# Windowed attention with expert routing: score columns outside a batch written by TensorE, gate product with the weights stationary

## The chip, the cores and the metric

One core of a Trainium2 chip runs the whole program in one launch. The core has TensorE (PE; its weight loads are listed apart, as PEld), VectorE (DVE), ScalarE (ACT), GpSimd (POOL) and SyncE (SP), which issues most transfers. The metric is the time of one execution on the device, in microseconds (us).

## The reference

Three stages follow each other. In the first, 4 batches of 8 heads attend over 576 positions, each position to itself and the 127 before it:

```python
scores = scale * np.matmul(q, k.transpose(0, 1, 3, 2))          # scale = 1/8, head_dim 64
mask = (rel >= 0) & (rel < 128)                                  # rel = query position - key position
scores = np.where(mask, scores + bias[None], -1000000000.0)      # bias = -slope[h] * |rel|
scores = scores - np.max(scores, axis=-1, keepdims=True)
attn = np.exp(scores); attn = attn / (np.sum(attn, axis=-1, keepdims=True) + 1e-09)
return np.matmul(attn, v)
```

In the second, each of the 2304 tokens (512 numbers) goes to two of 8 experts, chosen by a gate:

```python
noisy_logits = x @ w_gate + np.log1p(np.exp(x @ w_noise)) * noise   # w_gate, w_noise: 512 x 8
top2 = np.argpartition(-noisy_logits, 2, axis=1)[:, :2]             # weights: softmax over the two
out[mask] += top2_w[mask, k, None] * (np.maximum(x[mask] @ w1[e], 0.0) @ w2[e])
```

The third is `r = max(x @ w_in, 0)`, then `(r * r) @ w_out`, with 2048 columns in between.

## The kernel before, in words

**The attention stage** works on 18 tiles of 128 tokens (number i). A tile holds two blocks of 64 queries (x = 0, 1), and there are 9 blocks in a batch. A tile is done in two steps, g = 0 and 1, of four heads each (two pairs j of two heads a), which gives 36 steps, v = 2i + g. A step does this:

- `s_step`: TensorE writes the scores of 64 queries against up to 192 keys into a pair of PSUM banks (psb, L256). VectorE adds the bias and takes the row extremes, with the sign turned, in one operation per head (L266, with a small read of the accumulator behind it). ScalarE takes the exponential (L272).
- `t_step`: TensorE transposes the result (L283, into psa), ScalarE copies it out (L285).
- `pv_step`: TensorE multiplies by V (L307, into psb). VectorE divides by the row sums (`norm`, L318, L321, L324).

**At the edge of a batch** the first block has 64 keys and the second 128, not 192. A tile that holds such a block is treated by `parts`: VectorE fills the unused columns of the result with 1e9 (L262), and the operation L266 runs for each half of the partitions by itself, eight times in a step and not four. This concerns tiles 0, 4, 5, 9, 13 and 14, thus 12 of the 36 steps: v = 0, 1, 8 to 11, 18, 19 and 26 to 29.

**The order** is written out by hand. The loop runs `s_step(v + 2)`, `t_step(v + 1)`, the work of slot 4, `pv_step(v)` with `norm`, then the work of slot 5. Slots 0 to 3 lie between the four maxima of a step. Every engine takes its instructions in this order. The banks of psb exist twice and are taken in turn by scores and by products with V, so the scores of a step can start only when the maxima of the step before have been read.

**The gate** works on pairs of tiles (p = 0 to 8), one pair every four steps. `gate_t` transposes the tokens of a tile (L337, into the single bank psc, copied out by L339), `gate_m` multiplies them by the gate's weights, with the tokens as the stationary operand (L347: 8 products of fp32, 16 records in the trace). ScalarE and VectorE work out the noisy logits (L351 to L360), the two largest (L363, L366) and their one-hot rows (L370). `rank` counts the tokens ahead on TensorE (L382), `place` turns the counts into places (L392 to L418), and `scatter` writes the tokens' numbers to those places by indirect transfers from POOL (L424).

**The end of the stage**: the places of tiles 12 and 13 (p = 6) must be scattered before a first part of the table is read back (L497) and the first 3 x 128 rows of expert 0 are gathered (L437) and transposed (L444). In the meantime TensorE works through the last steps. Experts and feed-forward stage follow; their code is not touched.

Of the kernel before, what the change touches and what calls it, by code (L numbers as in the profile page):

```python
# [11 lines left out]
F32 = mybir.dt.float32  # L12
# [31 lines left out]
C_TRI = C_BIAS + H * 192  # L44
C_N = C_TRI + 128


@with_exitstack
def attn_moe_ffn(ctx: ExitStack, tc: tile.TileContext, qt, kt, vt, wgn, noise, w1, w2, w_in, w_out,
# [81 lines left out]
    bias = qp.tile([128, H, 192], F32, name="bias")  # L131
    wg_sb = qp.tile([128, 4, 16], F32, name="wg_sb")
    nz_sb = qp.tile([128, NT, 8], F32, name="nz_sb")
    trs = qp.tile([128, 128], F32, name="trs")
    tri = const.tile([128, 128], BF16, name="tri")
    ones = const.tile([128, 128], BF16, name="ones")
    acc = const.tile([128, 2, 8], BF16, name="acc")
    snap = const.tile([1, 2, 4], F32, name="snap")
# [67 lines left out]
    load_v(4)  # L206
    nc.gpsimd.memset(ones, 1.0)
    nc.gpsimd.memset(acc, 0.0)
    nc.gpsimd.memset(zero, 0)
    nc.gpsimd.dma_start(out=slot_tab, in_=zero)  # L210

    def more_consts():
        nc.vector.tensor_copy(iota8, cst[:, C_IO:C_IO + 8])
        nc.vector.tensor_copy(tok, cst[:, C_TOK:C_TOK + NT])
        nc.vector.tensor_copy(tri, trs)

# [12 lines left out]

    def parts(i):  # L230

        c = [max(128 - 64 * ((2 * i + x) % TB), 0) for x in range(2)]
        if c == [0, 0]:
            return [(0, 128, 0)]
        return [(0, 64, c[0]), (64, 128, c[1])]

    def s_step(v, now):
# [7 lines left out]
        ps = bank("b")[:, :, 0:384].rearrange("p a (j n) -> p a j n", j=2)  # L245
        p2, mx = [], []
        for j in range(2):
            p2.append(wk.tile([128, 2, 192], F32, name="p2", tag="p2", bufs=6))
            mx.append(wk.tile([128, 2], F32, name="mx", tag="mx", bufs=6))
            for x in range(2):  # L250
                b, t = divmod(2 * i + x, TB)
                k0 = max(64 * t - 128, 0)
                n = 64 * t + 64 - k0
                for a in range(2):
                    pa = slice(64 * a, 64 * a + 64)
                    nc.tensor.matmul(ps[64 * x:64 * x + 64, a, j, 192 - n:192],  # L256
                                     Q[i][pa, 2 * g + j, 64 * x:64 * x + 64], K[b][pa, 2 * g + j, k0:k0 + n],
                                     start=True, stop=True)
        for p0, p1, c0 in parts(i):
            if c0:  # L260
                for j in range(2):
                    nc.vector.memset(p2[j][p0:p1, :, 0:c0], 1.0e9)  # L262
        for j in range(2):
            for a in range(2):
                for p0, p1, c0 in parts(i):
                    nc.vector.tensor_tensor_reduce(  # L266
                        out=p2[j][p0:p1, a, c0:], in0=ps[p0:p1, a, j, c0:], in1=bias[p0:p1, 4 * g + 2 * j + a, c0:],
                        op0=OP.add, op1=OP.min, scale=-0.125, scalar=3.0e38, accum_out=mx[j][p0:p1, a:a + 1])
                run(now, 2 * j + a)
# [63 lines left out]
    def gate_t(i):  # L333
        ps = bank("c").rearrange("p (c n) -> p c n", c=4)
        xi = XI.pop(i)
        for c in range(4):
            nc.tensor.transpose(ps[:, c, :], xi[:, c * 128:(c + 1) * 128], ident)  # L337
        G["xt", i] = wk.tile([128, 4, 128], F32, name="xt", tag="xt", bufs=4)
        nc.scalar.activation(out=G["xt", i], in_=ps, func=AF.Copy)  # L339


    def gate_m(p):
        gp = bank("c")[:, 0:32].rearrange("p (q w) -> p q w", q=2)
        for q in range(2):
            xt = G.pop(("xt", 2 * p + q))
            for c in range(4):
                nc.tensor.matmul(gp[:, q, :], xt[:, c, :], wg_sb[:, c, :], start=(c == 0), stop=(c == 3))  # L347
        gs = wk.tile([128, 8, 2, 8], F32, name="gs", tag="gs", bufs=2)
# [38 lines left out]
    def place(p, n):  # L387
# [21 lines left out]
        elif n == 4:  # L409
            for q in range(2):  # L410
                for k in range(2):
                    nc.vector.tensor_tensor_reduce(out=gs[:, 6 + k, q], in0=oh[:, q, k, :], in1=t[:, q],
                                                   op0=OP.mult, op1=OP.max, scale=1.0, scalar=0.0,
                                                   accum_out=pf[:, q, k:k + 1])
        elif n == 5:
# [90 lines left out]
    for p in range(NT // 2):  # L506
# [3 lines left out]
        at(v + 1, 4, gate_t, 2 * p + 1)  # L510
        at(v + 2, 0 if end else 4, gate_m, p)
        o = v + 2 if end else v + 3
# [658 lines left out]
def _consts():  # L1171
    c = np.zeros((128, C_N), np.float32)
    c[:, C_ID:C_ID + 128] = np.eye(128)
    c[:, C_TRI:C_TRI + 128] = np.arange(128)[:, None] < np.arange(128)[None, :]
    r = np.arange(64)
    col = np.arange(192)
# [14 lines left out]
def _layout(inputs):  # L1191
# [8 lines left out]
    vt = np.stack([vp[:, 64 * s:64 * s + 128] for s in range(10)], axis=2)  # L1200
    wgn = np.concatenate([f["moe_w_gate"], f["moe_w_noise"]], axis=1).reshape(4, 128, 16).transpose(1, 0, 2)
    noise = f["moe_noise"].reshape(NT, 128, 8).transpose(1, 0, 2)
# [22 lines left out]
```

## Time and profile before

| | |
|---|---|
| time, three runs | 1016.82, 1016.60, 1014.82 us; median 1016.6 |
| span of the profiled execution | 1016.9 us, 0.3 above the median and 0.1 above the slowest of the runs |
| PE busy | 975.9 us (96%) |
| PEld busy | 895.6 us (88%) |
| DVE busy | 696.9 us (69%) |
| ACT busy | 465.3 us (46%) |
| POOL busy | 381.8 us (38%) |
| mean granted TensorE clock | 0.986 of 2.4 GHz |

The shares are means over the whole span. The change touches the attention stage alone, which ends at about 159 us, where TensorE turns to the experts' products. What matters is therefore read from stretches of that stage: how long TensorE takes from one step's scores to the next, and whom it waits for.

### The profile page before, as it was taken

Reading aid. Unit: us, or ns where it says so; the run is one execution under the profiler, and the core shown is the slowest. Engines: PE = TensorE matmul, PEld = TensorE weight load, DVE = VectorE, ACT = ScalarE, POOL = GpSimd, SP = SyncE. Lnnn points to the kernel's source line nnn. Section 1 sums busy time; section 2 is a strip of 40 time slices with the busy share of each in tenths; the row PEclk is TensorE's granted clock in tenths of the full one; section 3 lists DMA queues with packets and bytes.
Section 4 is the critical chain, followed back from the end, with each engine's and each line's share of the span. In section 5 each row is a group of like instructions: output and inputs, shape, how many; then the busy total and the mean of one; then the engine's idle time right before and its main releaser. Section 6 shows DMA issues by size and latency. Waiting matters only on the chain. (4 is left out here: it accounts for less than half of the span.)

```text
span 1016.9 us, 19557 instructions
## 1 busy us (share of the span) xinstructions
PE 975.9 (96%) x7432; PEld 895.6 (88%) x7432; DVE 696.9 (69%) x1608; ACT 465.3 (46%) x857; POOL 381.8 (38%) x374
## 2 busy tenths in 40 slices
PE   8899789999999999999999999999999989999998
PEld 5677668989898989989898897999999978999997
DVE  5777854547667566756765266887577899887773
ACT  5677652334434343433443245655554454443331
POOL 1544443212121031312121033625121649988880
PEclk9999998999999999999999999999999999999999
DMA  9676532465656574574645253765634653444431
GB/s 315 209 241 229 160 116 74 146 186 148 204 170 206 173 248 157 193 232 165 204 149 178 85 173 94 229 177 166 168 101 140 193 166 105 145 135 140 134 112 42
DMA packets 135733, 168.04 MB, mean 165 GB/s; under 512 B 9856, under 2 KB 96016, under 8 KB 135248
## 3 DMA queue, kind: packets, MB, share of 16 engines
q1 hardware_dynamic: 128160, 145.98, 45.6%
q0 software_dynamic: 7472, 20.76, 6.6%
q8 instruction: 59, 0.97, 0.4%
q14 instruction: 42, 0.34, 0.1%
HBM read 118.69 MB, written 48.01 MB: 164 GB/s over the span
## 5 line engine op out<-in xcount | busy, mean ns | idle before, releaser
L272 ACT ACTIVATE p<-p,mx 128x192 f32<-128x192 f32 x144 | 60.4, 452 | 45.8 <-DVE mx L266 44.0
L815 POOL TENSOR_TENSOR gs<-xb 128x256 f32<-128x256 f32 x72 | 71.1, 1007 | 16.4 <-DVE wc L815 7.8
L472 ACT ACTIVATE ha<-psa 128x384 fp32r<-128x384 f32 x64 | 31.3, 491 | 98.6 <-PE psa L468 97.1
L633 POOL TENSOR_TENSOR ex<-ex 128x512 f32<-128x512 f32 x16 | 20.8, 1301 | 146.4 <-DVE ex L631 146.4
L633 POOL TENSOR_TENSOR et<-ex,et 128x512 f32<-128x512 f32 x16 | 20.9, 1305 | 137.7 <-DVE ex L631 137.7
L473 DVE SCALAR_TENSOR_TENSOR ha<-psa,ha 128x384 fp32r<-128x384 f32 x64 | 35.3, 554 | 47.2 <-ACT ha L472 46.9
L654 POOL DMA_INDIRECT yr<-yg,pos x36 | 38.8, 1078 | 73.3 <-DVE ha L473 52.2
L266 DVE CUSTOM_DVE_ANT_0 p<-psb,bias 128x192 f32<-128x192 f32 (+3 forms) x192 | 58.2, 319 | 9.7 <-PE psb L256 7.5
L424 POOL DMA_INDIRECT slots<-tok,pos x36 | 35.2, 977 | 73.4 <-DVE rs L318 46.3
L468 PE MATMUL psa<-xa,wa 128*128 128x384 f32 x288 | 54.4, 338 | 0.3 <-DVE ha L473 0.3
L468 PE MATMUL psa<-xa,wc 128*128 128x384 f32 x288 | 53.1, 335 | 0.0
L734 PE MATMUL psb<-wa,ha 128*128 128x512 f32 x216 | 53.0, 396 | 0.0
L738 ACT ACTIVATE yo<-psb 128x512 f32<-128x512 f32 x38 | 22.7, 597 | 61.5 <-PE psb L734 41.3
L468 PEld LDWEIGHTS psa<-xa,wa 128*128 128x128 f32 x288 | 49.6, 189 | 1.4 <-DVE ha L473 0.6
L468 PEld LDWEIGHTS psa<-xa,wc 128*128 128x128 f32 x288 | 49.6, 188 | 0.2
L815 DVE TENSOR_TENSOR wc<-gs,wc 128x512 fp32r<-128x512 f32 x48 | 48.7, 1054 | 1.3 <-ACT wc L815 1.3
L734 PE MATMUL psb<-wb,ha 128*128 128x512 f32 x176 | 46.3, 397 | 0.0
L734 PEld LDWEIGHTS psb<-wa,ha 128*128 128x128 f32 x216 | 39.5, 188 | 7.7
L114 DVE TENSOR_TENSOR wa<-raw,wa 128x1024 fp32r<-128x1024 f32 x20 | 24.5, 1224 | 30.2 <-ACT wa L110 30.2
L437 POOL DMA_INDIRECT xr<-xd,gidx x40 | 38.4, 960 | 16.9 <-issue 10.9
L473 DVE SCALAR_TENSOR_TENSOR hb<-psa,hb 128x512 fp32r<-128x512 f32 x32 | 22.1, 691 | 32.7 <-ACT hb L472 32.7
L992 DVE SCALAR_TENSOR_TENSOR yo<-yo 128x384 f32<-128x384 f32 x48 | 43.2, 900 | 1.6
(302 smaller groups left out, 2724.9 us busy)
## 6 DMA issues: line engine op xcount, KB each, us to landing
raw<-in_w_dram SPq DMA_DIRECT2D x64, 512.0 KB, 5.4
xb<-gmid SPq DMA_DIRECT2D x72, 256.0 KB, 3.4
v<-in_vt_dram SPq DMA_DIRECT2D x20, 520.0 KB, 5.1
yg<-yo SPq DMA_DIRECT2D x40, 256.0 KB, 4.3
gmid<-yo SPq DMA_DIRECT2D x48, 192.0 KB, 2.1
ex<-in_w_in_dram SPq DMA_DIRECT2D x16, 512.0 KB, 4.9
ex<-in_w_out_dram SPq DMA_DIRECT2D x16, 512.0 KB, 4.3
xd<-xi SPq DMA_DIRECT2D x18, 256.0 KB, 2.6
```

The source lines that it names most:

```text
L266: nc.vector.tensor_tensor_reduce(out=p2[j][p0:p1, a, c0:], in0=ps[p0:p1, a, j, c0:], in1=bias[p0:p1, 4 * g + 2 * j + a, c0:], op0=OP.add, ...
L272: nc.scalar.activation(out=p2[j][:, a, :], in_=p2[j][:, a, :], func=AF.Exp, bias=mx[j][:, a:a + 1], scale=-1.0)
L424: st = nc.gpsimd.indirect_dma_start(out=slots, out_offset=bass.IndirectOffsetOnAxis(ap=pos[:, i, k:k + 1], axis=0), in_=tok[:, i:i + 1], i ...
L437: nc.gpsimd.indirect_dma_start(out=XR[e, j], out_offset=None, in_=xd[0:EARLY * 128] if early else xd, in_offset=bass.IndirectOffsetOnAxis( ...
L468: nc.tensor.matmul(o, w[wp][:, f * 128:(f + 1) * 128], x[:, xp, d, :], start=(n == 0), stop=(n == 11))
L472: nc.scalar.activation(out=hi, in_=ps, func=AF.Relu)
L473: nc.vector.scalar_tensor_tensor(out=lo, in0=ps, scalar=0.0, in1=hi.bitcast(F32), op0=OP.max, op1=OP.subtract)
L633: nc.gpsimd.tensor_tensor(out=cf, in0=af, in1=cf, op=OP.add)
L654: nc.gpsimd.indirect_dma_start(out=YR[i, k], out_offset=None, in_=yg, in_offset=bass.IndirectOffsetOnAxis(ap=pos[:, i, k:k + 1], axis=0))
L734: nc.tensor.matmul(py, h[:, hq], wc[wp][:, wsl], start=(f + n == 0), stop=(f == 7 and n == 2))
L815: f(**a)
L992: nc.vector.scalar_tensor_tensor(out=t, in0=t, scalar=0.0, in1=t, op0=OP.max, op1=OP.mult)
```

## The change

Three edits. **Score columns**: at the edge of a batch TensorE writes the unused columns too, by products of bfloat16 constants (64 rows of ones against columns of -1.25e8, thus -8e9 in each), two for each such block. VectorE no longer fills anything, and L266 runs over all 128 partitions and 192 columns in every step, four times. **Gate**: the weights, padded from 16 to 32 columns, become the stationary operand. Each of the four quarters of the 512 inputs goes to its own group of 32 columns of the array (`gate_w`, 256 tokens at a time), so that the four partial sums come out side by side on 128 partitions. VectorE copies them to SBUF, and `gate_m` adds them up with a product against a constant 128 x 16 matrix, which brings the tokens back to the partitions. `gate_w` stands in slot 4, where `gate_m` was, and `gate_m` in slot 5, behind the product with V. **Places**: the four fused multiply-and-maximum operations of `place` become one product and one maximum over 32 elements.

```diff
@@ tiles
-    wg_sb = qp.tile([128, 4, 16], F32, name="wg_sb")
+    wg_sb = qp.tile([128, 4, 32], F32, name="wg_sb")
-    trs = qp.tile([128, 128], F32, name="trs")
+    trs = qp.tile([128, 144], F32, name="trs")
+    far = qp.tile([128, 256], BF16, name="far")
...
+    nc.gpsimd.memset(far, -1.25e8)
@@ s_step
-    def parts(i):
-        c = [max(128 - 64 * ((2 * i + x) % TB), 0) for x in range(2)]
-        if c == [0, 0]:
-            return [(0, 128, 0)]
-        return [(0, 64, c[0]), (64, 128, c[1])]
...
+        for x in range(2):
+            c = max(128 - 64 * ((2 * i + x) % TB), 0)
+            if c:
+                for a in range(2):
+                    pa = slice(64 * a, 64 * a + 64)
+                    nc.tensor.matmul(ps[64 * x:64 * x + 64, a, :, 0:c], ones[pa, 0:64],
+                                     far[pa, 0:2 * c].rearrange("p (j n) -> p j n", j=2), start=True, stop=True)
...
-        for p0, p1, c0 in parts(i):
-            if c0:
-                for j in range(2):
-                    nc.vector.memset(p2[j][p0:p1, :, 0:c0], 1.0e9)
         for j in range(2):
             for a in range(2):
-                for p0, p1, c0 in parts(i):
-                    nc.vector.tensor_tensor_reduce(
-                        out=p2[j][p0:p1, a, c0:], in0=ps[p0:p1, a, j, c0:], in1=bias[p0:p1, 4 * g + 2 * j + a, c0:],
-                        op0=OP.add, op1=OP.min, scale=-0.125, scalar=3.0e38, accum_out=mx[j][p0:p1, a:a + 1])
+                nc.vector.tensor_tensor_reduce(
+                    out=p2[j][:, a, :], in0=ps[:, a, j, :], in1=bias[:, 4 * g + 2 * j + a, :],
+                    op0=OP.add, op1=OP.min, scale=-0.125, scalar=3.0e38, accum_out=mx[j][:, a:a + 1])
@@ gate_t, gate_w, gate_m
-        G["xt", i] = wk.tile([128, 4, 128], F32, name="xt", tag="xt", bufs=4)
-        nc.scalar.activation(out=G["xt", i], in_=ps, func=AF.Copy)
+        p, q = divmod(i, 2)
+        if q == 0:
+            G["xt", p] = wk.tile([128, 4, 2, 128], F32, name="xt", tag="xt", bufs=2)
+        nc.scalar.activation(out=G["xt", p][:, :, q, :], in_=ps, func=AF.Copy)
+
+    def gate_w(p):
+        xt = G.pop(("xt", p)).rearrange("p c q n -> p c (q n)")
+        ps = bank("c")[:, 0:256]
+        for c in range(4):
+            nc.tensor.matmul(ps[32 * c:32 * c + 32, :], wg_sb[:, c, :], xt[:, c, :], start=True, stop=True)
+        G["gt", p] = wk.tile([128, 256], F32, name="gt", tag="gt", bufs=1)
+        nc.vector.tensor_copy(G["gt", p], ps)
 
     def gate_m(p):
         gp = bank("c")[:, 0:32].rearrange("p (q w) -> p q w", q=2)
+        gt = G.pop(("gt", p))
         for q in range(2):
-            xt = G.pop(("xt", 2 * p + q))
-            for c in range(4):
-                nc.tensor.matmul(gp[:, q, :], xt[:, c, :], wg_sb[:, c, :], start=(c == 0), stop=(c == 3))
+            nc.tensor.matmul(gp[:, q, :], gt[:, q * 128:(q + 1) * 128], trs[:, 128:144], start=True, stop=True)
@@ place, n == 4
-            for q in range(2):
-                for k in range(2):
-                    nc.vector.tensor_tensor_reduce(out=gs[:, 6 + k, q], in0=oh[:, q, k, :], in1=t[:, q],
-                                                   op0=OP.mult, op1=OP.max, scale=1.0, scalar=0.0,
-                                                   accum_out=pf[:, q, k:k + 1])
+            prod = gs[:, 6:8].rearrange("p k q w -> p q k w")
+            nc.vector.tensor_tensor(out=prod, in0=oh, in1=t[:, :, None, :].to_broadcast([128, 2, 2, 8]), op=OP.mult)
+            nc.vector.tensor_reduce(out=pf, in_=prod, op=OP.max, axis=mybir.AxisListType.X)
@@ slots of the pairs
         at(v, 4, gate_t, 2 * p)
         at(v + 1, 4, gate_t, 2 * p + 1)
-        at(v + 2, 0 if end else 4, gate_m, p)
+        at(v + 2, 0 if end else 4, gate_w, p)
+        at(v + 2, 0 if end else 5, gate_m, p)
@@ constants: column sums of the four groups; gate weights padded to 32 columns
+    c[:, C_SUM:C_SUM + 16] = np.arange(128)[:, None] % 32 == np.arange(16)[None, :]
...
+    wgn = np.zeros((128, 4, 32), np.float32)
+    wgn[:, :, 0:8] = f["moe_w_gate"].reshape(4, 128, 8).transpose(1, 0, 2)
+    wgn[:, :, 8:16] = f["moe_w_noise"].reshape(4, 128, 8).transpose(1, 0, 2)
```

How the order of instructions moves is shown at three places. The first is VectorE at step v = 10 (tile 5, the first block with 128 of its 192 keys): p2_792 and p2_798 are the two results, psb_791 the scores, mx the row extremes. Before:

```order
L262 MEMSET p2_792 64x2x64
L262 MEMSET p2_798 64x2x64
L266 ISA p2_792,mx_793<-psb_791,bias_93 64x128
L266 ISA mx_793 64x1
L266 ISA p2_792,mx_793<-psb_791,bias_93 64x192
L266 ISA mx_793 64x1
L266 ISA p2_792,mx_793<-psb_791,bias_93 64x128
L266 ISA mx_793 64x1
L266 ISA p2_792,mx_793<-psb_791,bias_93 64x192
L266 ISA mx_793 64x1
```

These are the two fills and the first half of the maxima; as many follow for p2_798. With the change the same step has the whole of its maxima in eight rows:

```order
L264 ISA p2_778,mx_779<-psb_775,bias_93 128x192
L264 ISA mx_779 128x1
L264 ISA p2_778,mx_779<-psb_775,bias_93 128x192
L264 ISA mx_779 128x1
L264 ISA p2_784,mx_785<-psb_775,bias_93 128x192
L264 ISA mx_785 128x1
L264 ISA p2_784,mx_785<-psb_775,bias_93 128x192
L264 ISA mx_785 128x1
```

Two fills, four maxima and four reads of the accumulator are gone from this step. The second place is TensorE around the gate of the first pair, from the scores of step v = 7 to those of step v = 8 (xt: transposed tokens; wg_sb: the weights; x8 counts products). Before:

```order
L256 MATMUL psb<-k,q 64x192 x8
L283 MATMUL psa<-cst,p_481 128x128 x3
L283 MATMUL psa<-cst,p_487 128x128 x3
L347 MATMUL psc<-wg_sb,xt 128x16 x8
L307 MATMUL psb<-v,pt 64x65 x16
L256 MATMUL psb<-k,q 64x192 x2
```

And with the change, up to the same scores:

```order
L259 MATMUL psb<-k,q 64x192 x8
L281 MATMUL psa<-cst,p_475 128x128 x3
L281 MATMUL psa<-cst,p_481 128x128 x3
L346 MATMUL psc<-xt,wg_sb 32x256 x4
L305 MATMUL psb<-v,pt 64x65 x16
L354 MATMUL psc<-trs,gt 128x16 x2
L248 LDWEIGHTS ones
L248 MATMUL psb<-far,ones 64x2x128
L248 LDWEIGHTS ones
L248 MATMUL psb<-far,ones 64x2x128
L259 MATMUL psb<-k,q 64x192 x2
```

Eight products of 16 columns are replaced by four of 256 columns in front of the product with V and two of 16 columns behind it, and the fills of an edge step stand ahead of its scores. The third place is VectorE in the same step with the change: gt_576 is the copy of the partial sums, the rows above it are the last two maxima of the step, those below the division by the row sums.

```order
L264 ISA p2_545,mx_546<-psb_538,bias_93 128x192
L264 ISA mx_546 128x1
L348 COPY gt_576<-psc_571 128x256
L316 TENSOR_SCALAR rs_595<-psb_578 128x4
L319 RECIPROCAL rs_595<-rs_595 128x4
L322 TENSOR_TENSOR xi_533<-psb_578,rs_595 128x256
```

The copy is new, behind the maxima of its step and ahead of the division; before, VectorE went from the one to the other.

## Rows read from the trace of the kernel before

**Rows 1.** Busy time by stretch; columns: stretch, length, busy by engine, PEclk, DMA share, GB/s

```profile
...
31.40:51.20 19.80, 15.31 (x246) 11.99 (x239) 17.32 (x111) 10.69 (x25) 8.94 (x11) 0.91 0.50 163
72.10:85.18 13.08, 11.95 (x180) 9.52 (x181) 10.50 (x69) 9.59 (x24) 7.57 (x10) 0.87 0.46 143
88.52:102.63 14.11, 13.75 (x251) 11.18 (x251) 9.80 (x72) 10.70 (x29) 7.63 (x10) 1.00 0.80 278
102.63:126.44 23.81, 18.57 (x284) 14.51 (x287) 19.24 (x122) 15.52 (x39) 10.89 (x17) 0.93 0.51 153
36.50:39.90 3.40, 3.12 (x32) 2.35 (x30) 3.07 (x18) 1.70 (x5) 0.00 (x0) 0.50 0.51 206
149.10:159.30 10.20, 7.13 (x53) 5.66 (x53) 4.15 (x22) 2.76 (x5) 4.59 (x9) 0.50 0.24 72
175.00:1016.90 841.90, 821.49 (x5164) 771.83 (x5163) 579.06 (x824) 360.71 (x595) 311.18 (x273) 1.00 0.52 160
...
```

**Rows 2.** Timeline of TensorE, four regular steps: start, length, engine, line, operation

```profile
...
88.52 0.88 PE L256 MATMUL psb<-k,q 64*64 64x192 f32 x16 [0.17 <-PE psb L307]
...
91.74 0.83 PE L256 MATMUL psb<-k,q 64*64 64x192 f32 x16
...
95.95 0.83 PE L256 MATMUL psb<-k,q 64*64 64x192 f32 x16
...
99.30 0.88 PE L256 MATMUL psb<-k,q 64*64 64x192 f32 x16
...
```

**Rows 3.** Waits of TensorE, 0 to 165 us: total, times, longest

```profile
...
PE psb L256 <- DVE mx L266: 5.5, 7, 1.7
PE psc L382 <- DVE oh L370: 5.3, 7, 2.2
PE psa L444 <- DMA xr<-xd,gidx: 3.1, 1, 3.1
...
```

**Rows 4.** VectorE groups up to 240 us: busy, mean ns, idle before

```profile
...
L266 DVE CUSTOM_DVE_ANT_0 p<-psb,bias 128x192 f32<-128x192 f32 (+3 forms) x192 | 58.2, 319 | 9.7 <-PE psb L256 7.5
...
L266 DVE DVE_READ_ACCUMULATOR2_ANT mx<- 64x1 f32 (+1 forms) x192 | 15.4, 80 | 0.0
...
L262 DVE MEMSET p<- 64x256 f32 (+1 forms) x32 | 6.8, 218 | 0.8
...
```

**Rows 5.** VectorE groups up to 165 us, shapes apart

```profile
...
L266 DVE CUSTOM_DVE_ANT_0 p<-psb,bias 128x192 f32<-128x192 f32 x96 | 30.7, 352 | 2.4 <-PE psb L256 2.0
L324 DVE TENSOR_TENSOR xi<-psb,rs 128x256 f32<-128x256 f32 x36 | 15.3, 425 | 1.3
...
L266 DVE DVE_READ_ACCUMULATOR2_ANT mx<- 128x1 f32 x96 | 8.0, 83 | 0.0
...
L412 DVE CUSTOM_DVE_ANT_0 gs<-oh,gs 128x8 f32<-128x8 bf16 x32 | 3.4, 162 | 0.3
...
L370 DVE TENSOR_TENSOR oh<-iota,sel 128x32 bf16<-128x32 uint32 x9 | 1.7, 190 | 0.1
...
```

**Rows 6.** TensorE groups up to 165 us, shapes apart

```profile
...
L256 PE MATMUL psb<-k,q 64*64 64x192 f32 x448 | 30.1, 350 | 4.8 <-DVE mx L266 2.6 <-DMA q<-in_qt_dram 1.6 <-PE psb L307 0.2
...
L256 PE MATMUL psb<-k,q 64*64 64x64 f32 x64 | 3.8, 240 | 0.8 <-DVE mx L266 0.7
...
```

**Rows 7.** Timeline of TensorE around a regular gate product

```profile
...
61.97 0.88 PE L283 MATMUL psa<-cst,p 128*128 128x128 f32 x6
62.68 1.86 PE L347 MATMUL psc<-wg_sb,xt 128*128 128x16 f32 x16
64.47 1.13 PE L307 MATMUL psb<-v,pt 128*64 128x65 f32 x32
65.41 0.83 PE L256 MATMUL psb<-k,q 64*64 64x192 f32 x16
...
```

**Rows 8.** Timeline of the chain at the end of the stage

```profile
...
137.25 0.16 DVE L418 TENSOR_TENSOR pos<-gs,cst 128x4 int32<-128x4 f32 x1
...
150.59 0.69 PE L444 MATMUL psa<-cst,xr 128*128 128x128 f32 x2 [3.06 <-DMA xr<-xd,gidx]
...
```

More of the change, by code (lines that the diff above doesn't have):

```diff
@@ L44 @@
 C_TRI = C_BIAS + H * 192
-C_N = C_TRI + 128
+C_SUM = C_TRI + 128
+C_N = C_SUM + 16
 @with_exitstack
@@ L214, in more_consts @@
         nc.vector.tensor_copy(tok, cst[:, C_TOK:C_TOK + NT])
-        nc.vector.tensor_copy(tri, trs)
+        nc.vector.tensor_copy(tri, trs[:, 0:128])
     NV = 2 * NT
@@ L1200, in _layout @@
     vt = np.stack([vp[:, 64 * s:64 * s + 128] for s in range(10)], axis=2)
-    wgn = np.concatenate([f["moe_w_gate"], f["moe_w_noise"]], axis=1).reshape(4, 128, 16).transpose(1, 0, 2)
+    wgn = np.zeros((128, 4, 32), np.float32)
+    wgn[:, :, 0:8] = f["moe_w_gate"].reshape(4, 128, 8).transpose(1, 0, 2)
+    wgn[:, :, 8:16] = f["moe_w_noise"].reshape(4, 128, 8).transpose(1, 0, 2)
     noise = f["moe_noise"].reshape(NT, 128, 8).transpose(1, 0, 2)
```

## The prediction, made before the result was known

> **What bounds the kernel now.** I read the waits of TensorE first, because TensorE is busy 821.5 of the 841.9 us behind 175 us [rows 1]: nothing in that part is touched, so every microsecond that the attention stage gives up ahead of it should reach the end. In the attention stage TensorE waits mainly for VectorE: 5.5 us for row extremes before it may write the next scores, 5.3 us for the one-hot rows before it counts tokens, and 3.1 us once for gathered rows at the end [rows 3].
>
> Then I compared steps. TensorE's regular steps start at 88.52, 91.74, 95.95, 99.30 and 102.63 us [rows 1, 2], so four steps take 3.22 + 4.21 + 3.35 + 3.33 = 14.11 us. In them TensorE is busy 13.75 us, VectorE 9.80, ScalarE 10.70, at full clock [rows 1]: they are bound by TensorE. The three stretches with the edge of a batch are longer than the regular steps of the same kinds:
>
> - 31.40 to 51.20, four steps: 19.80 against 14.11, so 5.69 more.
> - 72.10 to 85.18, three steps: 13.08 against 3.22 + 4.21 + 3.35 = 10.78, so 2.30 more.
> - 102.63 to 126.44, five steps: 23.81 against 14.11 + 3.22 = 17.33, so 6.48 more.
>
> Together they lose 14.5 us. VectorE is busy 17.32 of 19.80 and 19.24 of 23.81 us there, TensorE only 15.31 and 18.57 [rows 1], so VectorE bounds them. The idle time costs twice: from 36.50 to 39.90 us the granted clock was 0.50, thus 1.2 and not 2.4 GHz [rows 1].
>
> **Score columns.** All maxima in the stage take 58.2 us, their reads 15.4, the fills 6.8; of these the 96 full operations take 30.7 and their reads 8.0 [rows 4, 5]. The split ones with their fills thus take (58.2 - 30.7) + (15.4 - 8.0) + 6.8 = 41.7 us. In their place come 48 full ones at (30.7 + 8.0) / 96 = 0.40 us, together 19.4. VectorE loses 22.3 us, or 1.86 in each of the 12 edge steps. For the first stretch that makes 17.32 - 4 x 1.86 = 9.9 us, plus 0.4 for the copy below, in four steps: as much as the 9.80 of regular steps, in which TensorE sets the pace. So I expect the edge steps to fall to the regular pace, and the 14.5 us to go. I keep back 2.0 of them: TensorE still waits a little for VectorE before each counting, and a 1.2 GHz stretch of 3.4 us that stays, or appears elsewhere in dense work, costs half its length, 1.7 us. That gives 12.5 us. The two edge steps at the start (tile 0) I count at nothing, since loads follow at once.
>
> The fills move to TensorE. A column of an fp32 score record costs (350 - 240) / 128 = 0.86 ns, from the 192- and 64-column records [rows 6]. No row shows a bfloat16 product of this shape; at the fp32 price as a bound, 256 columns take 0.22 us and 128 take 0.11. The block with unused columns has less score work in its half of the array: four records of 64 columns take 0.22 us in each quarter, against 0.66 for the four of 192 in the other half, so 0.22 + 0.22 still ends first. Between nothing and 2.0 us (six steps at 0.22, six at 0.11, in a row with the scores) I take 0.05 in each of 10 steps, 0.5 us.
>
> **Gate.** In a regular pair the products start at 62.68 and the product with V behind them at 64.47 [rows 7]: 1.79 us, for 16 records that follow at 1.86 / 16 = 0.116 us although each moves only 16 columns. Now 8 records of 256 columns move 0.22 us each, 1.76 us in a row. The question is whether the four column groups run beside each other. No row has groups of 32 columns. The nearest is the scores, in four quarters of the array: 16 records of 192 columns would take 16 x 0.165 = 2.64 us in a row and 1.32 if only the halves of the rows overlapped, but the block takes 0.83 [rows 2, 6]. So groups of columns do run beside each other, at least 3.2 at once. For `gate_w` the bounds are 0.44 (four at once) and 1.76 us (none); I take 1.76 / 3.2 = 0.55. The adding product has four records at 0.116, 0.47 us.
>
> The new products use other parts of the array than their neighbours, which has a price. Transposes and gate products of the same form overlap by 62.85 - 62.68 = 0.17 us, gate products and the product with V, of another form, by 64.54 - 64.47 = 0.07 [rows 7]: a change of form costs about 0.1 us. One more of them comes in front of the product with V and two behind it, 0.3 us. The pair takes 0.55 + 0.47 + 0.3 = 1.32 us against 1.79, a gain of 0.47. The Trainium skill ("TensorEngine Tiling (Array Packing)", Key Properties) says that a change of tiling mode, not merely of the tile, drains the engine. That speaks against this edit, and the lost 0.1 us agrees with it; a full drain of the 0.17 us overlap at each of the three would leave 0.26 us of the gain. The same skill ("TensorE: Matmul & The Clock Gate", Part 3) gives three groups of 32 columns a speedup of 2.38, which no run here shows; an estimate from it for four groups is 3.2 too.
>
> The gain counts for seven pairs (p = 0 to 6), 7 x 0.47 = 3.3 us, with bounds 7 x 0.58 = 4.1 us and a loss of 7 x 0.74 = 5.2. For pair 7 it is lost: the places of pair 6 are ready at 137.25, their scatter, the read of the table and the gather end at 150.59, and TensorE has then waited 3.06 us for the rows [rows 8]. What TensorE saves in that time lengthens the wait. Pair 8 runs `gate_w`, copy and `gate_m` without anything in between; its stall of about 0.5 us eats its gain.
>
> **The new wait.** `gate_m` waits for the copy, and behind it stand the next scores and all else on TensorE. The copy costs at most 0.43 us, like the 128 x 256 operation L324 [rows 5], and VectorE has 4.3 us idle in four regular steps. The scores of the step end about when the transposes start, at 61.97; four maxima make that 63.6, the copy 64.0. TensorE would come to `gate_m` after `gate_w` (63.2) and the product with V, which takes 65.41 - 64.47 = 0.94 [rows 7], at 64.2. So the cover is 0.2 us thick; if it fails, the stall is a few tenths per pair and the 3.3 us are gone.
>
> **Places.** Four operations of 0.16 us that overlap become two of about 0.19 (like L370) that wait for each other [rows 5]. I count nothing, between 0.3 us saved and 0.1 lost on VectorE for each pair, hidden by the same idle time.
>
> **Sum.** 12.5 - 0.5 + 3.3 = 15.3 us off the span of 1016.9 us, 1001.6; the span is 0.3 above the median of the runs, so 1001.3 us.
>
> **Rivals.**
>
> - *The column groups don't overlap.* The gate then costs 5.2 us, and the sum is 12.5 - 0.5 - 5.2 = 6.8: 1009.8 us. For it: no row with 32 columns, and the start of one record in a group must wait for the last one there. Against it: the scores.
> - *Half of the edge loss stays*, because the chain from scores over maxima and exponential to the transposes, with a clock that still falls, holds the step: 7.2 - 0.5 + 3.3 = 10.0, 1006.6 us. For it: ScalarE, next in that chain, has 10.70 of 14.11 us to do even in regular steps [rows 1]. Against it: regular steps hold their pace with the same work.
> - *The end takes it all.* If the first gather hung on something that doesn't come earlier (the scatters of POOL, queued behind weights that it prepares from loads), TensorE would arrive early and wait: 1016.6 us, no change. Against it: POOL is busy 10.89 of 23.81 us in the last edge stretch [rows 1], so it can follow.
> - *Slower: lockstep at the gate.* `gate_m` stands in TensorE's queue ahead of the next scores. If VectorE comes to the copy only after late maxima, TensorE waits for up to four maxima and a copy, 1.6 + 0.4 = 2.0 us, and VectorE then waits for scores. Nine pairs make 18 us; the clock stood at 0.50 behind such a pause [rows 1, 3], which in four of them costs 4 x 1.7 = 6.8. With 15.3 saved elsewhere that gives 1026 us. It decides from 1.7 us of stall per pair. Against it: the 0.2 us of cover above, and that VectorE has least to do in this step.
>
> **How the numbers follow.** The forecast has 0.69, its own range is 996 to 1005 us. The overlap failing has 0.10, half of the edge loss 0.12, the end 0.05, lockstep 0.04. If all 14.5 us go, the gate gains 4.1, the fills cost nothing and the 1.2 GHz stretch from 149.10 to 159.30 [rows 1] gets shorter by a third, 1.7 us, the time is 996; a little more at the start could make 994.5. To hold 8 in 10 the range goes from there to 1010. What a measurement here can tell from no change is 0.2%, 2 us: faster 0.91, same 0.05, slower 0.04.
>
> **What would show it.** Steps at 3.2 to 3.6 us through the edge stretches, at clock 1.00, with VectorE under 80% busy; fewer than 3 us of waits for maxima. The block of `gate_w` at 0.5 to 0.7 us (1.8 or more: no overlap), no wait of `gate_m` for the copy, and a wait of some 3.5 us for the gathered rows. I am wrong if edge steps still take over 4 us, or if the gate's step does not fall below 4.2.

## The result and the profile after

The changed kernel took 1001.36 us in the median of four runs (1001.12 to 1003.35), the kernel before 1016.71 beside it: a ratio of 0.9847, with a 95% interval of 0.9829 to 0.9866. The forecast was 1001.3 us. One of the four runs of the kernel before took 5322.31 us; it is among the four of the median, but the ratio goes by the fast runs alone.

The profiled execution of the changed kernel has a span of 999.3 us and took 1001.12 us; in each of its four runs the time lies about 1.8 us above the span. The span of before, 1016.9 us, is already above its slowest run, so if as much lay around it, the execution profiled there took 1018.7 us, 2.1 above the median. The spans therefore differ by 17.6 us and the medians by 15.3.

Busy time by stretch, of the changed kernel, cut at the starts of the same steps as before [rows 1]. The columns are the same: stretch, length, busy time and instructions of PE, PEld, DVE, ACT and POOL, granted clock, DMA share, GB/s.

```profile
...
29.12:43.12 14.00, 13.16 (x239) 9.97 (x238) 10.83 (x66) 10.80 (x28) 7.87 (x11) 1.00 0.70 225
43.12:64.00 20.88, 19.82 (x366) 15.17 (x367) 16.51 (x109) 15.18 (x40) 9.43 (x12) 1.00 0.76 260
64.00:74.38 10.38, 9.66 (x185) 7.38 (x181) 7.32 (x46) 8.28 (x23) 7.57 (x10) 1.00 0.53 166
...
77.68:91.42 13.74, 13.34 (x249) 10.11 (x249) 10.34 (x66) 10.76 (x29) 7.60 (x10) 1.00 0.86 304
...
91.42:108.24 16.82, 16.23 (x287) 12.36 (x290) 12.40 (x78) 13.94 (x37) 10.02 (x15) 1.00 0.54 183
...
130.10:140.30 10.20, 7.14 (x53) 5.66 (x53) 4.10 (x16) 2.77 (x5) 5.24 (x10) 0.50 0.31 96
...
```

The first, third and fifth row are the stretches with the edge of a batch. They took 19.80, 13.08 and 23.81 us and now take 14.00, 10.38 and 16.82: 15.49 us less. VectorE was busy 87%, 80% and 81% of them; it is now busy 77%, 71% and 74%, and TensorE 93 to 96%. The four regular steps (fourth row) take 13.74 us, not 14.11. Up to 130 us the changed kernel is at full clock. Before, each of the three edge stretches had a time at 1.2 GHz: beside 36.50 to 39.90 these are 80.8 to 84.3 and 121.8 to 125.2, where the granted clock was 0.50. The half-clock stretch at the end stays, as long as it was.

What TensorE waits for in the first 165 us, to be read against [rows 3] (columns: who waits, for what, total, times, longest):

```profile
PE psa L449 <- DMA xr<-xd,gidx: 3.3, 1, 3.3
PE psc L389 <- DVE oh L377: 3.3, 7, 0.8
...
PE psc L354 <- DVE gt L348: 0.5, 1, 0.5
...
```

The 5.5 us of waits for row extremes are gone. The wait before counting fell from 5.3 to 3.3 us, the wait for gathered rows is about as long as it was (3.1 and 3.3), and `gate_m` (L354) waits for the copy (L348) once, in the last pair.

### The profile page after: what moved, and what is told of

Its sections match the earlier page's. It is cut to its first block, busy times and chain, and to the rows that moved or that the text cites. A ratio compares the mean times of both kernels' runs of the same rounds, so it can differ in the third digit from the quotient of the medians.

```text
span 999.3 us, 19373 instructions
## 1 busy us (share of the span) xinstructions
PE 963.9 (96%) x7428; PEld 880.9 (88%) x7428; DVE 680.5 (68%) x1435; ACT 463.0 (46%) x857; POOL 382.4 (38%) x375
## 5 line engine op out<-in xcount | busy, mean ns | idle before, releaser
L821 POOL TENSOR_TENSOR gs<-xb 128x256 f32<-128x256 f32 x72 | 72.9, 1032 | 17.6 <-DVE wc L821 7.8
L270 ACT ACTIVATE p<-p,mx 128x192 f32<-128x192 f32 x144 | 57.6, 451 | 28.4 <-DVE mx L264 27.6
L264 DVE CUSTOM_DVE_ANT_0 p<-psb,bias 128x192 f32<-128x192 f32 x144 | 45.8, 351 | 14.5 <-PE psb L259 12.4
L442 POOL DMA_INDIRECT xr<-xd,gidx x40 | 38.3, 958 | 17.4 <-issue 11.2
```

Of the source, the lines that this page charges most:

```text
L264: nc.vector.tensor_tensor_reduce(out=p2[j][:, a, :], in0=ps[:, a, j, :], in1=bias[:, 4 * g + 2 * j + a, :], op0=OP.add, op1=OP.min, scale= ...
L270: nc.scalar.activation(out=p2[j][:, a, :], in_=p2[j][:, a, :], func=AF.Exp, bias=mx[j][:, a:a + 1], scale=-1.0)
L442: nc.gpsimd.indirect_dma_start(out=XR[e, j], out_offset=None, in_=xd[0:EARLY * 128] if early else xd, in_offset=bass.IndirectOffsetOnAxis( ...
L821: f(**a)
```

## Experiments

The experiments fall into three sets. Each set ran on one chip and shares its runs of the kernel before. That kernel took 1051.7 us on the chip of the first set (`e1`, `e2`, `e3` and the first `e10`), 1043.8 on that of the second (`e0`, `e4`, `e8` and the second `e10`) and 1017.4 on that of the third (`e5`, `e6`, `e11`, `e12`), so ratios are compared, and microseconds only within a set; the last experiments come back to the reason. The edits are shown shortened.

**Which part of the score edit matters: `e8_split_kept`.** The changed kernel, TensorE's fills included, but the maxima of the edge steps in two halves again:

```diff
-                nc.vector.tensor_tensor_reduce(out=p2[j][:, a, :], ...)
+                edge = any(max(128 - 64 * ((2 * i + x) % TB), 0) for x in range(2))
+                for p0, p1 in ((0, 64), (64, 128)) if edge else ((0, 128),):
+                    nc.vector.tensor_tensor_reduce(out=p2[j][p0:p1, a, :], ...)
```

> The changed kernel, with its unused columns written by TensorE, but the maxima of the edge steps still in two operations of 64 partitions (each now over all 192 columns). It separates the two parts of the edge's gain. VectorE then has 8 operations at about 0.36 + 0.08 us in an edge step, 3.2 us with their gaps and not 1.2 to 1.6, and loses only the fills (0.57 us a step). Theory (VectorE's whole load in the step counts): about 9 to 12 us slower than the changed kernel, edge stretches above the regular pace by 3 to 5 us each. Rival (the fills, which stand ahead of the first maximum, were what held the step): no more than 3 us slower.

Measured: ratio 0.9982, interval 0.9954 to 1.0009; 1042.36 us against 1030.95 for the changed kernel in the same set, 11.4 more. Scores on TensorE in its first two edge steps (start, length, engine, line, operation, operands, idle time before):

```profile
31.20 0.87 PE L259 MATMUL psb<-k,q 64*64 64x192 f32 x16
...
36.64 0.30 PE L248 MATMUL psb<-far,ones 64*64 64x256 bf16 x2 [0.42 <-DVE mx L266]
36.65 1.01 PE L259 MATMUL psb<-k,q 64*64 64x192 f32 x16
...
42.28 0.24 PE L248 MATMUL psb<-far,ones 64*64 64x128 bf16 x2 [0.94 <-DVE mx L266]
42.30 0.87 PE L259 MATMUL psb<-k,q 64*64 64x192 f32 x16
```

and two of the split maxima, the last of the first step and the first of the second, on VectorE:

```profile
36.22 0.36 DVE L266 CUSTOM_DVE_ANT_0 p<-psb,bias 64x192 f32<-64x192 f32 x1
...
37.73 0.35 DVE L266 CUSTOM_DVE_ANT_0 p<-psb,bias 64x192 f32<-64x192 f32 x1
```

The steps are 5.45 and 5.65 us long, as before the change (5.61 and 5.78), and TensorE waits for the extremes again. Half the partitions take 0.35 us, as long as all 128: the split doubled VectorE's time for the maxima. In this set the whole change is worth 12.9 us, and 11.4 of them go when the split comes back: the edge loss was the split, not the fills on VectorE, and removing it brings the gain.

**The score edit alone: `e1_scores_only`.** The kernel before with the new `s_step`; gate and places as they were.

```diff
-        for p0, p1, c0 in parts(i):   # fills on VectorE, maxima in halves
+        for x in range(2):            # fills on TensorE, then one maximum per head
```

> Only the edit of the score columns; gate and places as before. Theory (VectorE bounds the edge steps, and nothing else holds them): the three edge stretches fall to the pace of regular steps, 14.5 us, and some 1 to 2 us at the start where edge steps stand too; no half-clock stretch between 30 and 130 us; 1016.6 - 15 = about 1001.5 us, ratio about 0.985. Rival (the gate's edit shares the edges' gain, because the gate's products stand in the same stretches): about half, 1008 us, ratio 0.992.

Measured: 0.9861 (0.9826 to 0.9896), 15.3 us less than before on that chip. The whole change gave 0.9847 and 0.9884 in two other sets of runs, so the score edit alone gives as much as the interval can tell, and the rival's 0.992 lies outside it. That the stretches fall to the regular pace can't be read from this run: TensorE has 13 us of waits in it that the last experiments are about.

**The other parts.** `e2_gate_only` is the kernel before with the new gate, `e3_places_only` with the new `place`, `e4_scores_and_places` the changed kernel with the old gate, `e0_after_again` the changed kernel once more.

```diff
e2  -  at(v + 2, 4, gate_m, p)
    +  at(v + 2, 4, gate_w, p); at(v + 2, 5, gate_m, p)
e3  -  four fused tensor_tensor_reduce in place, n == 4
    +  tensor_tensor (mult) and tensor_reduce (max)
e4  -  gate_w and gate_m of the change
    +  gate_m of the kernel before, in slot 4
```

> Only the edit of the gate; score columns and places as before. Theory: a gate step gets 0.47 us shorter and the counting step behind it 0.17 us longer, so 0.3 for each of the four pairs outside the edge stretches, and at the edges the copy adds 0.43 us to the engine that bounds them: a net of 0 to 1.5 us gained, 1015 to 1016.6 us. Rival (the prediction's own term): 3.3 us gained, 1013.3 us, ratio 0.9967. Rival (the new wait hurts): slower than before.

> Only the edit of the places. Theory: two dependent operations of 0.19 us last as long as four overlapping ones of 0.16, so no change: 1016.6 us within 1. Rival (four operations and four reads fewer on VectorE in each pair free the edge steps): 1 to 2 us faster.

> The changed kernel with the gate of before. Theory (the gate's edit is worth 0.47 us in the gate's step, less 0.17 in the counting step, for seven pairs): about 2 us slower than the changed kernel, gate steps at 4.2 us and counting steps at 3.36. Rival (the prediction's term): 3.3 us slower. Rival (the gate's edit gives nothing, or costs): as fast as the changed kernel, or faster.

> The changed kernel itself, as the measure for the other three of this group. Both theories: ratio 0.985 to before where TensorE has its instructions in time; on a chip where it waits for them (entries 'issue' in the waits of TensorE) a few tenths of a per cent lower or higher.

Measured: gate only 0.993 (0.9906 to 0.9954), places only 1.0006 (0.9966 to 1.0045), scores and places 0.9878 (0.984 to 0.9916), the changed kernel 0.9884 (0.9841 to 0.9927). No effect of the places shows, but the interval reaches some 4 us either way, so the rival's 1 to 2 us is not excluded. The gate's worth can't be read from these runs. By `e2_gate_only` it is 7.9 us, more than the theory and either rival allowed for; by the changed kernel against `e4_scores_and_places` it is 1.0 us in the medians and a loss of 0.6 by the ratios. The gate steps of `e4_scores_and_places`, expected at 4.2 us, take 4.27 to 8.53 on that chip. The gate's worth is read from its step in the third set, with the next run.

**Do the column groups run beside each other: `e5_one_group`.** All four quarters into one group of 32 columns, one after the other:

```diff
-            nc.tensor.matmul(ps[32 * c:32 * c + 32, :], wg_sb[:, c, :], xt[:, c, :], start=True, stop=True)
+            nc.tensor.matmul(ps[0:32, :], wg_sb[:, c, :], xt[:, c, :], start=(c == 0), stop=(c == 3))
```

The copy and the adding product then work on 32 partitions.

> The changed kernel with the four quarters of the gate's inputs added up in one group of 32 columns instead of side by side in four. Theory (the four groups run beside each other, which is what made the gate's step 0.47 us shorter): the block of gate_w, 0.57 us with four groups, takes 8 x 0.22 = 1.76 us, the gate's step 3.74 + 1.2 = 4.9 us, and nine pairs cost 8 to 11 us against the changed kernel, whose ratio was 0.985 on one chip and 0.988 on another: ratio 0.993 to 1.000. Rival (the gain comes from fewer and longer records, whatever the groups): block under 0.9 us, gate's step under 4.1 us, ratio as the changed kernel's.

Measured: 0.9945 (0.9924 to 0.9965). TensorE around a gate product in the changed kernel (start, length, operation):

```profile
54.12 0.88 PE L281 MATMUL psa<-cst,p 128*128 128x128 f32 x6
54.93 0.64 PE L346 MATMUL psc<-xt,wg_sb 128*32 128x256 f32 x8
55.50 1.13 PE L305 MATMUL psb<-v,pt 128*64 128x65 f32 x32
56.56 0.62 PE L354 MATMUL psc<-trs,gt 128*128 128x16 f32 x4
57.10 0.88 PE L259 MATMUL psb<-k,q 64*64 64x192 f32 x16
```

and the same place with one group:

```profile
57.51 0.87 PE L281 MATMUL psa<-cst,p 128*128 128x128 f32 x6
58.31 1.91 PE L346 MATMUL psc<-xt,wg_sb 128*32 128x256 f32 x8
60.16 1.13 PE L305 MATMUL psb<-v,pt 128*64 128x65 f32 x32
```

From the first gate product to the product with V it is 55.50 - 54.93 = 0.57 us with four groups and 1.85 with one, 3.2 times as long. The gate's step goes from 3.74 to 5.01 us, above the 4.21 of before, and the kernel takes 11.1 us more than the next one here, which ran in the same set with the gate as changed. The groups overlap, and without that the gate edit would be a loss. The rival, that fewer and longer records gave the gain whatever the groups, falls.

**What a fill costs: `e6_fills_x5`.**

```diff
-                for a in range(2):
+                for a in (0, 1) * 5:
```

> The changed kernel with every fill of unused score columns issued five times. Theory (a fill lies beside the scores of the other half of the array and costs TensorE about 0.05 us per step): the edge steps grow by 0.1 to 0.3 us each, together 1 to 4 us, ratio 0.986 to 0.992. Rival (fills run one after the other with the scores, 0.22 us for 256 columns): four more of them add 0.9 us to a step with 256 columns and 0.4 to one with 128, together 8 us over twelve steps, ratio 0.992 to 0.998.

Measured: 0.9836 (0.9802 to 0.9871). Its first edge step on TensorE (start, length, operation):

```profile
29.02 0.41 PE L248 MATMUL psb<-far,ones 64*64 64x256 bf16 x4
29.17 0.38 PE L259 MATMUL psb<-k,q 64*64 64x192 f32 x2
29.27 0.38 PE L248 MATMUL psb<-far,ones 64*64 64x256 bf16 x4
29.38 0.33 PE L259 MATMUL psb<-k,q 64*64 64x192 f32 x2
29.48 0.27 PE L248 MATMUL psb<-far,ones 64*64 64x256 bf16 x2
29.54 0.49 PE L259 MATMUL psb<-k,q 64*64 64x192 f32 x12
29.97 0.87 PE L281 MATMUL psa<-cst,p 128*128 128x128 f32 x6
```

and that of the changed kernel:

```profile
29.11 0.30 PE L248 MATMUL psb<-far,ones 64*64 64x256 bf16 x2
29.12 0.87 PE L259 MATMUL psb<-k,q 64*64 64x192 f32 x16
29.91 0.88 PE L281 MATMUL psa<-cst,p 128*128 128x128 f32 x6
```

Fills and scores stand between each other. From the first fill to the transposes it is 0.95 us, against 0.80 with one set: four more sets cost 0.15 us, so one set, here two records, costs about 0.04. Steps 18 and 19 (tile 9, both blocks) have four records in a set; there it is 0.98 and 0.96 us against 0.70 and 0.61, so 0.07 to 0.09 for a set. The theory holds for the size of a fill. The whole kernel's ratio lies below the 0.986 to 0.992 that it expected: it did not get slower by anything its interval can show. The rival, 8 us, falls.

**A wait on VectorE that the change brought: `e10_weights_earlier`, run on two chips.** In the regular steps of the changed kernel the gate's step is 0.47 us shorter (3.74), but the counting step behind it went from 3.35 to 3.52. The scores of three regular steps, the gate's, the counting one and the next:

```profile
80.90 0.83 PE L259 MATMUL psb<-k,q 64*64 64x192 f32 x16
...
84.64 0.88 PE L259 MATMUL psb<-k,q 64*64 64x192 f32 x16
...
88.16 0.88 PE L259 MATMUL psb<-k,q 64*64 64x192 f32 x16
```

VectorE's first gate operation (L365, between SBUF tiles) had grown. First VectorE, then POOL, both of the changed kernel (start, length):

```profile
58.44 0.29 DVE L365 TENSOR_TENSOR gs<-gs,nz_sb 128x16 f32<-128x16 f32 x1
58.77 0.17 DVE L367 TENSOR_TENSOR gs<-gs,psc 128x16 f32<-128x16 f32 x1
```

```profile
56.35 2.35 POOL L115 TENSOR_TENSOR wa<-raw,wa 128x1024 fp32r<-128x1024 f32 x1
```

L365 ends at 58.73, POOL's subtraction at 58.70. In seven of nine pairs L365 starts while that subtraction runs, takes 0.29 to 0.72 us and ends 0.02 to 0.04 us behind it; in the other two it takes 0.18, and before the change it never took more. The steps became shorter, POOL's chain of scatters and weights didn't. Two kernels of the third set, described above and below, show the same place with one group, whose steps are longer, and with the scatters apart, whose subtraction (57.87 to 60.22) lies over L367, the same operation there:

```profile
63.10 0.17 DVE L365 TENSOR_TENSOR gs<-gs,nz_sb 128x16 f32<-128x16 f32 x1
```

```profile
59.84 0.41 DVE L367 TENSOR_TENSOR gs<-gs,nz_sb 128x16 f32<-128x16 f32 x1
```

What this operation takes beyond 0.17 us the counting step takes too. Outside the edges (steps 12, 16, 24 and 32) the step is 3.40 to 3.41 us with 0.17 in `e5_one_group` and `e12_no_scatters`; in the changed kernel it is 3.52 with 0.29 and 3.72 with 0.49, and in `e11_scatters_apart` 3.63 with 0.41.

The edit starts the weights a step later in the program, between the scatters of two tiles, and so ahead of the next L365 (hence "earlier" in its name):

```diff
-            if v % 4 == 2 and nprep[0] < 8:
+            if v % 4 == 3 and nprep[0] < 8:
```

> The changed kernel with one edit: POOL's preparation of an expert weight stands one step earlier (after step v % 4 == 3, not 2), so that it is done before VectorE's first gate operation. In the changed kernel that operation (L365) ends, in 7 of 9 pairs, within 0.03 us of the end of POOL's subtraction. Theory (VectorE's operation waits for POOL's, which lies over it): L365 falls from a mean of 0.35 us to 0.17, the counting steps from 3.52 to about 3.36, and the kernel gains about 7 x 0.17 = 1.2 us on the changed kernel: about 1000.2 us. Rival (the counting step is longer because the gate's product comes after the product with V, and its logarithm later): L365 or the wait behind it stays, counting steps stay at 3.5.

> The changed kernel with POOL's preparation of weights one step earlier, beside the changed kernel on the same chip. Theory: 1.2 us faster than the changed kernel (ratio to it 0.9988); counting steps at about 3.36 us and L365 at 0.17. Rival: the same time as the changed kernel, since the counting step waits for something else.

Measured: 0.9724 (0.9688 to 0.976) and 0.9752 (0.9718 to 0.9786), 13.2 us below the changed kernel in the set that had both. L365 takes 0.17 us in all pairs. But in `e0_after_again`, the changed kernel on the same chip, it takes 0.17 in eight of nine pairs too (0.51 in the first), so L365 can't explain more than 0.3 us there. The expected counting steps of 3.36 us did not come either: in `e10_weights_earlier_again` four of seven take 4.54 to 4.72. The gain has another source. On those two chips TensorE has waits of a kind that neither profile ahead of this section has. The changed kernel there, in `e0_after_again`, 0 to 165 us (who waits, for what, total, times, longest):

```profile
PE psb L259 <- issue: 6.9, 10, 1.0
PE psb L305 <- issue: 4.3, 11, 0.4
```

and `e10_weights_earlier_again` on the same chip:

```profile
PE psb L259 <- issue: 1.3, 2, 0.9
...
PE psb L305 <- issue: 0.9, 3, 0.3
```

"Issue" means that TensorE waited for nothing the profile shows. In `e0_after_again` these waits stand behind the first scatters of a pair (POOL, then TensorE):

```profile
52.32 0.99 POOL L429 DMA_INDIRECT slots<-tok,pos  x1 [7.71 <-DVE rs L316]
...
56.17 0.96 POOL L429 DMA_INDIRECT slots<-tok,pos  x1 [0.21 <-issue]
```

```profile
54.34 1.11 PE L305 MATMUL psb<-v,pt 128*64 128x65 f32 x27
55.84 0.33 PE L305 MATMUL psb<-v,pt 64*64 64x65 f32 x4 [0.39 <-issue]
56.57 0.21 PE L305 MATMUL psb<-v,pt 64*64 64x65 f32 x1 [0.39 <-issue]
...
57.98 1.57 PE L259 MATMUL psb<-k,q 64*64 64x192 f32 x14 [0.86 <-issue]
```

Four scatters run from 52.3 to 57.1 us; the waits begin at the third, and the clock then falls to half until 61.3. Regular steps that take 3.22 and 3.74 us in the first profile took 4.53 and 6.69 here. Parting the scatters by the weights took most of these waits away. Not all: in `e10_weights_earlier_again` the counting steps 12, 20, 28 and 32 are the four of 4.54 to 4.72 us, and in the first of them VectorE starts its first maximum late beside the second pair of scatters:

```profile
42.11 1.00 POOL L429 DMA_INDIRECT slots<-tok,pos  x1 [0.15 <-issue]
...
43.41 0.97 POOL L429 DMA_INDIRECT slots<-tok,pos  x1 [0.22 <-issue]
```

```profile
45.09 0.36 DVE L264 CUSTOM_DVE_ANT_0 p<-psb,bias 128x192 f32<-128x192 f32 x1 [1.58 <-PE psa L281]
```

The scores it reads stood complete at about 43.6, when TensorE had gone on to the transposes.

**Are the scatters the cause: `e11_scatters_apart` and `e12_no_scatters`.** In the first the second tile's scatters wait for the last maximum of their step, and the weights stay where they are; the second issues none, so the experts work on wrong rows.

```diff
e11 -            nc.gpsimd.memset(spacer, 0.0)
    +            nc.gpsimd.tensor_copy(spacer, MX[w][0:1, 1:2])   # first scatter of a pair's second tile
e12 -    def scatter(i): ... two indirect transfers per tile
    +    def scatter(i): pass
```

> The changed kernel, with the two scatters of a pair's second tile held back by one small POOL operation that reads the last maximum of its step; the preparation of weights stays where it is. Theory (four scatters one behind the other hold up TensorE's issue on some chips, and the version with weights prepared between them gained 13 us because it parted them): TensorE's waits put down to issue fall from 10 us to under 4, steps 3 and 0 of each group of four from 4.5 and 6.5 to under 4.2, time 8 to 13 us under the changed kernel's: ratio 0.972 to 0.980. Rival (that version gained because VectorE's first gate operation no longer lies over the weights' subtraction): that overlap stays here, so no gain, ratio 0.984 to 0.993. On a chip like the first, where no such waits are, both expect 0.985.

> The changed kernel without the scatters, so that the table of places stays at zero and the experts work on wrong rows. Theory (the scatters hold up TensorE's issue on some chips): no wait of TensorE put down to issue, all regular steps at 3.2 to 3.8 us, step 35 starts at 122 to 125 us on any chip; where the changed kernel needs 149 us for that, the time falls by 20 to 26 us to a ratio of 0.962 to 0.970. Rival (the late issue on those chips has another cause, as the loads or the fetching of instructions): the long steps stay, ratio 0.98 to 0.99.

Measured: 0.9833 (0.9799 to 0.9868) and 0.9795 (0.9759 to 0.9831). The kernel before took on this chip what it took ahead of the prediction, and the runs show no such waits (but for 0.3 us once in `e12_no_scatters`): step 35 starts at 124.06 and 121.77 us, against 122.13 in the profile after. So `e11_scatters_apart` says nothing on the question, and `e12_no_scatters` only what scatters cost on a quiet chip. It loses the wait for gathered rows, and its counting steps, with L365 at 0.17 us again, take 3.40 us. That the scatters hold up TensorE's issue on some chips is an inference from where the waits stand and from `e10_weights_earlier`, and is not shown; the rival named with `e12_no_scatters`, loads or instructions that come late there, was not tested. Which chips, and through what, stays open.

## Why the prediction was right, point by point

**Edge steps: 12.5 us forecast.** Right in mechanism, too careful in size. The three stretches gained 15.49 us. They now take 41.20 us, and as many regular steps of the changed kernel take 41.18 (four, three and five steps at 13.74, 10.48 and 16.96): all of the 14.5 lost went, with the fills already paid. The 2.0 us kept back for waits and a half-clock stretch were not needed, since both went. Single steps lie between 3.11 and 3.86 us, a little outside the 3.2 to 3.6 that were to show it; the longest, 3.86, has L365 at 0.72. `e8_split_kept` shows the cause.

**Fills: -0.5 us.** The 0.05 us per step stands: `e6_fills_x5` gives 0.04 where two records of 256 columns are written and 0.07 to 0.09 in the two steps with four records, and the edge now runs at the regular pace with them in it.

**Gate: 3.3 us.** The gain of a regular gate step is the forecast 0.47 us, and the block of `gate_w` took 0.57 where 0.55 was expected. That it fits so well is in part luck. The 3.2 at once came from scores that lie in two halves of the rows by two of the columns; no row showed four column groups. And the order has two changes of form more than before, not three. Each costs what was estimated, 0.10 us behind the transposes (54.93 - 54.12 against 62.68 - 61.97) and 0.12 behind the product with V (56.56 - 55.50 against 65.41 - 64.47); the third 0.1 went into the two new blocks, 0.57 and 0.54 us where 0.55 and 0.47 were expected. The trace does not bear out the full drain by the Trainium skill ("TensorEngine Tiling (Array Packing)", Key Properties), which would have left 0.26 us of gain and not 0.47.

The step that failed is the multiplication by seven as if nothing else moved. L365's wait for POOL is 0.12 to 0.55 us in the seven pairs, 1.64 together, and lengthens the counting step by as much; without it that step would be at 3.40, up to 0.05 above its 3.35 of before, for which nothing is shown. Of the 3.3 us some 1.3 to 1.7 are left, and in this profile less: the first pair's gate step took 4.30 us, not 3.74, since its transposes waited 0.49 us for the copy of the tokens. The prediction priced what TensorE and VectorE do in the step, and not what POOL does beside VectorE once steps are shorter.

**New wait, places, end.** `gate_m` waited once, for 0.5 us, in the last pair, where the prediction had a stall; lockstep did not come. No effect of the places shows in `e3_places_only`. The chain at the end moved up as a whole:

```profile
118.72 0.16 DVE L423 TENSOR_TENSOR pos<-gs,cst 128x4 int32<-128x4 f32 x1
...
131.58 1.11 PE L449 MATMUL psa<-cst,xr 128*128 128x128 f32 x4 [3.35 <-DMA xr<-xd,gidx]
```

The places are ready 18.5 us earlier than in [rows 8] and the rows 19.0; the wait grew from 3.06 to 3.35 us, where 3.5 was expected. The rival in which the end takes it all falls.

**The sum: 15.3 us.** That the forecast time was hit to 0.1 us is luck: the edge gave more than its term, the gate less, and outside the sum stand three more shifts of 1.4 to 2.3 us. The first product of the experts came 19.0 us earlier (158.81 to 139.80). Of this 2.28 lie ahead of step 8 and were counted at nothing. Kernels with the start of the changed one reach step 8 anywhere from 28.96 to 30.78 us. Most of it is a stretch at 1.2 GHz behind a wait for loads, from 12.6 to 16.0 us in the profile before, where step 2 takes 3.94 us; the profile after does not have it and step 2 takes 2.40; `e11_scatters_apart` and `e5_one_group`, with the new start, have it too, so it is spread between executions rather than the change. The other 16.7 are the three edge stretches (15.49), the regular ones (0.75) and the end (0.49). Behind the stage the program took 1.4 us longer, 859.5 against 858.1, in code that did not change; the executions of one kernel differ by 2, and nothing explains it further. And the prediction set the span of before against the median as if nothing lay around it; there are 1.8 us, so that its base was an execution 2.1 us above the median.

## What to carry to other kernels

Halving an operation over partitions halves nothing: on VectorE both halves cost a full one (0.35 us for 64 and for 128 partitions here), so let an engine with time to spare pad the data and keep the operation whole. A stretch bound by one engine fell to the pace of the next here when that engine was relieved, and all of its excess went; don't keep a part back without a row that says what would hold it. When steps get shorter, look at what keeps its own length beside them (here POOL's 2.35 us subtraction): it will lie over something that it used to miss.

## What the runs showed of the hardware

- Four groups of 32 columns with fp32 operands run 3.2 times as fast as one (0.57 against 1.85 us for 8 records of 256 columns). The prediction's estimate from three groups' 2.38 in the Trainium skill ("TensorE: Matmul & The Clock Gate", Part 3) came to the same.
- A VectorE operation that reads two SBUF tiles waited for the end of POOL's running subtraction, and ended 0.02 to 0.04 us behind it in each of seven pairs; the next one, with an operand in PSUM, kept its 0.17 us. The Trainium skill ("SBUF — State Buffer", SBUF: two separate sides) has the two engines share a pair of ports as an exclusive lock, for such operations too; the trace agrees.
- The same kernel before took 1017 us in two sets of runs and 1044 and 1052 in two others, on other chips. In profiles from those chips TensorE starts late for no shown reason while several indirect transfers are issued in a row (11.2 us in `e0_after_again`), and falls to half clock behind it (from 58.0 to 61.3 us there); that the transfers are the cause is not shown. Moving the weights between the scatters was worth 13 us there; on a quiet chip that version wasn't run.
